# A fused attention and channel-mix kernel: first chunk's mixed gate inputs on ScalarE and GpSimd, first loads and due dates anew

## The chip, the cores and the metric

The kernel runs on one core of a Trainium2 chip. The metric is the device time of one execution in microseconds; lower is better. The kernel before takes 631.29 us (median of three runs, 630.67 to 632.04). The engines have the profile's names: PE is TensorE's matmul, PEld its weight load, DVE is VectorE, ACT is ScalarE, POOL is GpSimd, SP the engine that issues the DMAs.

## The reference

Inputs are q, k and v of shape (8, 8, 576, 64) (batch, heads, tokens, head size) and the weights of the second part. All is float32.

```python
k_p = k.reshape(B, H, 72, 8, 64).mean(axis=3)        # keys and values: means of 8 tokens
v_p = v.reshape(B, H, 72, 8, 64).mean(axis=3)
attn = softmax(q @ k_p.T / 8)                        # sum + 1e-9 below
x = (attn @ v_p) as (8, 576, 512)                    # heads side by side
xk = mu_k * x + (1 - mu_k) * x_prev                  # x_prev: the token before, 0 for the first
xr = mu_r * x + (1 - mu_r) * x_prev
s = maximum(xk @ w_k, 0) ** 2                        # 512 -> 1024
out = sigmoid(xr @ w_r) * (s @ w_v)                  # 512 -> 512, and 1024 -> 512
```

## The kernel before, in words

The 4608 tokens of the eight batches are cut into 12 chunks of 384, and each chunk into 3 tiles of 128 tokens (36 tiles). For every tile there is `softmax` (scores of four head pairs on PE at L620, their maximum, exponential and sum, and the products px and pm of exponentials and inverse sums; pm has 64 keys of each head, px the last 8), then `transposed` (pm, L695) and `transposed_rest` (px, L740). For every chunk follow `attended` for the four 128-wide slices g of x (L794: values times weights into a bank, with the tile of transposed weights pth and the rest ptr), `shifted` inside it (L807: ACT copies the bank twice, scaled by 1 - mu, one column to the right into t; GpSimd brings the carried column; L826: VectorE makes mu * bank + t), `hidden` for the eight 128-wide parts of the k multiply (L870, then relu on ACT at L880, the square), `gate` (L919, sigmoid at L926) and `mixed` (L951, the v multiply, multiplied with the gate at L960 and stored).

Chunk 0 is "whole": its multiplies take float32 operands, L826 writes straight into the operands xkh (for the k multiply, m = 0) and xrh (for the gate, m = 1). Later chunks split every operand into a high and a low half (`x_parts`: ACT casts at L842, GpSimd subtracts at L844; for weights `split`, L491 and L494) and multiply three times.

The weights come as 64-bit words and are converted to float32 by `convert`: one step on ACT (L460), three on VectorE (L462 a shift, L464, L469). There are 8 for k, 4 for r, 8 for v: the names wk0 to wk7, wr0 to wr3, wv0 to wv7. Keys and values are summed over 8 tokens in one of three ways by the table SUM_BY: "t" by 8 matmuls with the identity (L512, 16 records), "v" by three halving additions on VectorE and "g" by the same on GpSimd (both L501). k0 and k1 are the halves of batch 0's keys, v0 and v1 of its values, r0 their last 8 keys; k2, k3, v2, v3, r1 are those of batch 1. The q tiles are q0, q1 and so on. LOADS gives the order of the first loads; one SP queue issues them all, and with some eight under way each waits for an earlier one.

What runs when is set while the program is written: all these steps are threads with a due time, and a planner with rough costs of its own (class Order) picks for each engine the earliest due step that could start. EARLIER shifts the due time of single threads of the first chunks by some microseconds. The result is a fixed order on each engine; each engine works off its own queue in order, and a step that waits holds up all behind it. Scores have one double bank (sc), except tile 1 (BESIDE), which uses two of the three mm banks. Tiles in BY_HEAD have their exponentials made head by head on ACT with bias and sum in the same instruction (L642, eight each); for others VectorE subtracts the maximum (L651), ACT makes one exponential (L656), and VectorE sums (L658). Sigmoid and exponential need different tables on ACT; where they alternate the program has an ACT_TABLE_LOAD between them.

## Time and profile before

| | before |
|---|---|
| median of 3 runs | 631.29 us |
| lowest, highest | 630.67, 632.04 us |
| profiled execution | 631.28 us |
| its span, first to last instruction | 629.5 us |
| TensorE matmul busy | 615.7 us |
| VectorE, ScalarE, GpSimd busy | 402.1, 354.6, 208.2 us |
| ACT_TABLE_LOAD | 24, 1.28 us each |

The profile is of one execution on the chip. 631.28 is that execution's time and 629.5 the span of its instructions, so 1.8 us lie around the span. Busy time of PE is rough: a matmul's end is modelled, and records of matmuls that follow each other overlap. In a row of the timeline the first number is the start in microseconds from the span's start, the second the time that the row's instructions cover, and in square brackets stands how long the engine was idle ahead of it and what ended that. A row of the waits view gives who waited for whom: sum in microseconds, number of waits, longest. A row of the windows view gives a stretch, its length, the busy time (and the instructions) of PE, PEld, DVE, ACT and POOL, the clock granted to TensorE as a share of full speed, and the DMA engines' busy share and GB/s. A row of the groups gives the sum in microseconds, the mean in ns, and the idle time before. A float32 matmul has two records.

### The profile page before, as it was taken

The page shows a single profiled execution, that of the slowest core. Times are in us where ns is not written, and L with a number is a line of the kernel's source. Part 1 is how long each engine was busy: PE and PEld are TensorE (multiplying, and loading weights), DVE is VectorE, ACT ScalarE, POOL GpSimd, SP SyncE. Part 2 cuts the span into 40 slices and gives each one's busy share as a digit, 9 for nine tenths or more (in the row PEclk, how much of TensorE's full clock was granted, in tenths as well). Part 3 has the DMA queues.
Part 4 walks back from the last instruction along what each step waited for, and adds up shares of the span by engine and source line. Part 5 has one row for each costly group of instructions (what it writes and reads, how often), then busy time and mean ns, then how long its engine had stood idle before and what let it go on. Part 6 is the DMA issues. An engine that isn't in the chain of part 4 may idle for free.

```text
span 629.5 us, 8993 instructions
## 1 busy us (share of the span) xinstructions
PE 615.7 (98%) x3210; PEld 533.1 (85%) x3210; DVE 402.1 (64%) x786; ACT 354.6 (56%) x778; POOL 208.2 (33%) x324
## 2 busy tenths in 40 slices
PE   6899999999999999999999999999999999999997
PEld 5755459889889989989989988988988988988986
DVE  5999977857787458657735765844884643663421
ACT  4776666765675645645555564545575545564420
POOL 1130266453453048029024017305346005113100
PEclk9999999999999999999999999999999999999999
DMA  9995101123314211033001151001330100000001
GB/s 315 340 403 171 34 35 51 35 76 142 94 51 158 59 51 51 2 143 108 18 18 51 42 187 55 3 18 56 133 98 33 35 18 33 18 2 33 18 2 50
DMA packets 34989, 50.92 MB, mean 81 GB/s; under 512 B 6528, under 2 KB 22912, under 8 KB 34944
## 3 DMA queue, kind: packets, MB, share of 16 engines
q1 hardware_dynamic: 34944, 50.35, 23.9%
q8 instruction: 25, 0.41, 0.3%
q14 instruction: 20, 0.16, 0.1%
HBM read 40.90 MB, written 9.44 MB: 80 GB/s over the span
## 4 chain that ended last, share of the span: by engine, by line
PE 88%; DMA 6%; DVE 5%; SPq 1%; issue 0%; DVEq 0%
PE mm L951 32%; PE mm L870 29%; PE mm L919 14%; PE bank L794 5%; PE sc L620 5%; DMA got_wk<-in_w_k 4%; PE bank L695 2%; DMA got_wv<-in_w_v 1%; DVE tmp L464 1%; DVE got_wr L469 1%; PE bank L750 1%; SPq L421 0%; DVE got_wv L469 0%; DVE tmp L462 0%; DVE ptl L708 0%
## 5 line engine op out<-in xcount | busy, mean ns | idle before, releaser
L870 PE MATMUL mm<-xkh,w_k 128*128 128x384 f32 x704 | 182.3, 339 | 0.0
L951 PE MATMUL mm<-w_v,sh 128*128 128x512 f32 x528 | 171.7, 393 | 0.0
L870 PEld LDWEIGHTS mm<-xkh,w_k 128*128 128x128 f32 x704 | 125.6, 188 | 1.5 <-issue 0.6
L870 PE MATMUL mm<-xkl,w_k 128*128 128x384 f32 x352 | 118.0, 335 | 0.0
L951 PEld LDWEIGHTS mm<-w_v,sh 128*128 128x128 f32 x528 | 99.3, 188 | 19.5
L951 PE MATMUL mm<-w_v,sl 128*128 128x512 f32 x264 | 103.1, 390 | 0.0
L919 PE MATMUL mm<-w_r,xrh 128*128 128x512 f32 x264 | 86.3, 397 | 0.0
L807 ACT ACTIVATE t<-bank,om_sb 128x384 f32<-128x384 f32 x96 | 49.1, 580 | 46.7 <-PE bank L794 46.6
L893 ACT CAST sh<-rk 128x384 fp32r<-128x384 f32 x88 | 45.2, 513 | 51.9 <-DVE rk L887 51.4
L670 POOL TENSOR_TENSOR px<-e,sm 128x64 f32<-128x64 f32 x31 | 9.6, 310 | 189.8 <-DVE sm L664 189.8
L960 DVE TENSOR_TENSOR rs<-mm,rs 128x512 f32<-128x512 f32 x36 | 24.7, 687 | 74.7 <-PE mm L951 74.6
L826 DVE SCALAR_TENSOR_TENSOR xm<-bank,mu_sb,t 128x384 f32<-128x384 f32 x88 | 51.1, 612 | 31.8 <-POOL t L819 15.4
L895 DVE TENSOR_TENSOR sl<-rk,sh 128x384 fp32r<-128x384 f32 x88 | 53.3, 610 | 21.3 <-ACT sh L893 21.2
L870 PEld LDWEIGHTS mm<-xkl,w_k 128*128 128x128 f32 x352 | 66.1, 188 | 0.0
L887 DVE SCALAR_TENSOR_TENSOR rk<-mm,rk 128x384 f32<-128x384 f32 x88 | 48.5, 552 | 22.7 <-ACT rk L880 21.9
L501 POOL TENSOR_TENSOR stage<-stage 128x512 f32<-128x512 f32 (+5 forms) x60 | 52.9, 887 | 25.5 <-DMA stage<-in_vm 14.8
L844 POOL TENSOR_TENSOR xkl<-xm,xkh 128x384 fp32r<-128x384 f32 x44 | 45.5, 1034 | 48.0 <-ACT xkh L842 47.6
L919 PEld LDWEIGHTS mm<-w_r,xrh 128*128 128x128 f32 x264 | 49.7, 188 | 10.1
L951 PEld LDWEIGHTS mm<-w_v,sl 128*128 128x128 f32 x264 | 49.7, 188 | 8.9
L880 ACT ACTIVATE rk<-mm 128x384 f32<-128x384 f32 x88 | 42.9, 487 | 22.1 <-PE mm L870 21.1
L919 PE MATMUL mm<-w_r,xrl 128*128 128x512 f32 x132 | 51.5, 390 | 0.0
L620 PE MATMUL sc<-kbd,qs 128*128 128x144 f32 (+1 forms) x312 | 40.6, 289 | 5.4 <-ACT e L642 3.2
(120 smaller groups left out, 952.8 us busy)
## 6 DMA issues: line engine op xcount, KB each, us to landing
out<-rs SPq DMA_DIRECT2D x36, 256.0 KB, 2.0
stage<-in_kT SPq DMA_DIRECT2D x15, 576.0 KB, 4.9
qs<-in_qT SPq DMA_DIRECT2D x32, 256.0 KB, 3.3
stage<-in_vm SPq DMA_DIRECT2D x14, 512.0 KB, 5.4
got_wk<-in_w_k SPq DMA_DIRECT2D x8, 512.0 KB, 10.0
got_wv<-in_w_v SPq DMA_DIRECT2D x8, 512.0 KB, 10.1
stage<-in_vr SPq DMA_DIRECT2D x7, 384.0 KB, 4.2
got_wr<-in_w_r SPq DMA_DIRECT2D x4, 512.0 KB, 9.7
```

The lines of the kernel that those rows point to most:

```text
L501: nc_eng.tensor_tensor(out=st[:, :, :w], in0=st[:, :, :w], in1=st[:, :, w:2 * w], op=ALU.add)
L620: nc.tensor.matmul(out=halves[g // 2][o:o + n, 0, k:k + 2 * KEYS], lhsT=qs[:, g, o:o + n], rhs=kbd[b % 2][:, g, :], start=True, stop=True,)
L807: nc.scalar.activation(out=t[:, m, 1:n + 1], in_=xp, func=AF.Copy, scale=om_sb[:, m, g:g + 1])
L826: nc.vector.scalar_tensor_tensor(out=xm[:, :n], in0=xp, scalar=mu_sb[:, m, g:g + 1], in1=t[:, m, :n], op0=ALU.mult, op1=ALU.add,)
L844: nc.gpsimd.tensor_tensor(out=lo, in0=xm[:, :n], in1=hi, op=ALU.subtract)
L870: nc.tensor.matmul(out=hp, lhsT=w[:, o], rhs=x[:, ct, :n], start=(ct == 0 and k == 0), stop=(ct == NCT - 1 and k == len(terms) - 1),)
L880: nc.scalar.activation(out=rk[:, :n], in_=hp, func=AF.Relu)
L887: nc.vector.scalar_tensor_tensor(out=rk[:, :n], in0=hp, scalar=0.0, in1=rk[:, :n], op0=ALU.max, op1=ALU.mult)
L893: nc.scalar.copy(out=sh[:, :n], in_=rk[:, :n])
L895: nc.vector.tensor_tensor(out=operand("sl", c)[:, jt, :n], in0=rk[:, :n], in1=sh[:, :n], op=ALU.subtract)
L919: nc.tensor.matmul(out=bank, lhsT=x[:, ct, o], rhs=w, start=(ct == 0 and k == 0), stop=(ct == NCT - 1 and k == len(terms) - 1),)
L951: nc.tensor.matmul(out=bank, lhsT=s[:, o], rhs=w, start=(jt == 0 and k == 0), stop=(jt == NJT - 1 and k == len(terms) - 1),)
```

## The change

In chunk 0 (SCALED_ON_ACT) the mixed input of the gate, m = 1, is no longer one VectorE instruction: ACT writes mu * bank into xrh, and GpSimd adds t to it in place. The bank is given back after ACT's step, t after GpSimd's. BY_HEAD takes in tile 1, so all three tiles of chunk 0 have their exponentials by head. In SUM_BY k1 goes from VectorE to GpSimd, v0 from TensorE to VectorE, v2 from GpSimd to TensorE, r1 from GpSimd to VectorE. LOW_BY deals the low halves of the weights anew (k: one more on GpSimd, v: one less). LOADS has another order: k1 ahead of k0, q0 behind q1 and q2, the small constants ahead of wk0, r0, k3, q5 and k2 at other places. EARLIER, SPARE and SECOND (due times) are new throughout; of EARLIER's some 200 numbers two stand below.

```diff
 LOADS = (
-    "k0 k1 q1 q0 q2 wk0 c0 v0 v1 wk1 k3 r0 wk2 q3 wk3 wk4 v3 wk5 r1 q4 v2 wk6 wk7 wr0 wr1 q5 k2 wr2 "
+    "k1 k0 q1 q2 q0 c0 wk0 v0 r0 wk1 wk2 v1 k3 wk3 q3 wk4 r1 wk5 wk6 q4 v3 v2 q5 wk7 k2 wr0 wr1 wr2 "
     "wr3 wv0 wv1 wv2 wv3 wv4 wv5 wv6 wv7 "
 )
 SUM_BY = {
-    "k0": "t", "k1": "v", "v0": "t", "v1": "t", "r0": "t", "k2": "v", "k3": "v", "v2": "g", "v3": "v",
-    "r1": "g",
+    "k0": "t", "k1": "g", "v0": "v", "v1": "t", "r0": "t", "k2": "v", "k3": "v", "v2": "t", "v3": "v",
+    "r1": "v",
 }
-LOW_BY = {"k": "gvgvvvgv", "r": "gvgv", "v": "gvvggvgv"}
-BY_HEAD = (0, 2)
+LOW_BY = {"k": "gvgvvggv", "r": "gvvg", "v": "gvvvgvvg"}
+BY_HEAD = (0, 1, 2)
+SCALED_ON_ACT = (0,)
 EARLIER = {
-    "transposed_rest 6": 4.1, "hidden 2 5": -6.4, "convert r 1": -3.5, "mixed 0 1": -9.9,
+    "transposed_rest 6": -1.8, "hidden 2 5": -23.9, "convert r 1": -2.2, "mixed 0 1": -10.7,
...
-SPARE = 2.4
-SECOND = 13.3
+SPARE = 3.5
+SECOND = 12.9
...
-            yield "dve", 0.15 + n / 960, False
-            nc.vector.scalar_tensor_tensor(
-                out=xm[:, :n], in0=xp, scalar=mu_sb[:, m, g:g + 1], in1=t[:, m, :n],
-                op0=ALU.mult, op1=ALU.add,
-            )
-            if m == ms[-1] and last:
+            if m and c in SCALED_ON_ACT:
+                yield act(n)
+                nc.scalar.activation(out=xm[:, :n], in_=xp, func=AF.Copy, scale=mu_sb[:, m, g:g + 1])
+                order.give("bank", bank)
+                yield pool(n)
+                nc.gpsimd.tensor_tensor(out=xm[:, :n], in0=xm[:, :n], in1=t[:, m, :n], op=ALU.add)
                 order.give("t", t)
-                order.give("bank", bank)
+            else:
+                yield "dve", 0.15 + n / 960, False
+                nc.vector.scalar_tensor_tensor(
...
```

After the change the lines stand 2 later up to L826, and 11 later from the new branch on: L642 is L644, L651 is L653, L870 is L881, L926 is L937.

What this moves is seen in the order of the built program. First, ScalarE's queue from the first weight to the first tile's ptr. Before:

```order
L460 ACTIVATE tmp_102<-got_wk_138 128x512
L642 ACTIVATE e_88,sm_98<-sc_112,mx_96 128x72 x8
L656 ACTIVATE e_89<-e_89 128x576
L460 ACTIVATE tmp_101<-got_wk_155 128x512
L642 ACTIVATE e_88,sm_98<-sc_112,mx_96 128x72 x8
L747 CAST ptr_270<-bank_115 96x2x128
```

And now:

```order
L462 ACTIVATE tmp_102<-got_wk_142 128x512
L644 ACTIVATE e_88,sm_98<-sc_112,mx_96 128x72 x8
L644 ACTIVATE e_89,sm_99<-mm_118,mx_97 128x72 x4
L644 ACTIVATE e_89,sm_99<-mm_116,mx_97 128x72 x4
L583 CAST vq_100<-mm_117 96x128
L554 COPY vbd_w<-stage_108 64x2x64 x2
L644 ACTIVATE e_88,sm_98<-sc_112,mx_96 128x72 x8
L749 CAST ptr_289<-bank_115 96x2x128
```

Tile 1's single exponential became eight by head, and the second weight no longer stands between the tiles.

Second, TensorE from the last scores of the opening to the fourth slice of chunk 0's x. L512 sums values with the identity, L794 is `attended`, L870 (now L881) the k multiply; mm and bank are its banks. Before:

```order
L794 MATMUL bank_113<-pth_308,vbd_w 128x384
L794 MATMUL bank_113<-ptr_270,vbd_r_76 128x384
L870 MATMUL mm_117<-xkh_361,got_wk_165 128x384
L870 MATMUL mm_118<-xkh_361,got_wk_138 128x384
L794 MATMUL bank_115<-pth_308,vbd_w 128x384
L794 MATMUL bank_115<-ptr_270,vbd_r_76 128x384
L870 MATMUL mm_117<-xkh_361,got_wk_165 128x384
L870 MATMUL mm_118<-xkh_361,got_wk_138 128x384
```

And now:

```order
L796 MATMUL bank_115<-pth_295,vbd_w 128x384
L796 MATMUL bank_115<-ptr_289,vbd_r_76 128x384
L881 MATMUL mm_116<-xkh_362,got_wk_142 128x384 x2
L881 MATMUL mm_118<-xkh_362,got_wk_152 128x384 x2
L796 MATMUL bank_114<-pth_295,vbd_w 128x384
L796 MATMUL bank_114<-ptr_289,vbd_r_76 128x384
L796 MATMUL bank_113<-pth_295,vbd_w 128x384
L796 MATMUL bank_113<-ptr_289,vbd_r_76 128x384
L514 MATMUL mm_117<-stage_107,ident 128x128 x8
L881 MATMUL mm_116<-xkh_362,got_wk_142 128x384
```

Four k multiplies go ahead of the third slice, the third and fourth slices stand together, and the sums of v2 behind them. On VectorE there stand, ahead of the first mixed input (L837), the nine steps of weights 1, 2 and 4 and of softmax 3 (L464 three times, L466 and L471 twice each, a maximum L635 and a subtraction L653).

Third, ScalarE at the gates of chunk 0, where rs is the sigmoid's result and e an exponential's. Before:

```order
L460 ACTIVATE tmp_102<-got_wv_330 128x512
L926 ACT_TABLE_LOAD
L926 ACTIVATE rs_78<-mm_118 128x512
L460 ACTIVATE tmp_101<-got_wv_322 128x512
L926 ACTIVATE rs_79<-mm_116 128x512
L747 CAST ptr_457<-bank_113 96x2x128
```

And now:

```order
L462 ACTIVATE tmp_102<-got_wv_318 128x512
L937 ACT_TABLE_LOAD
L937 ACTIVATE rs_78<-mm_118 128x512
L658 ACT_TABLE_LOAD
L658 ACTIVATE e_88<-e_88 128x576
L462 ACTIVATE tmp_101<-got_wv_345 128x512
L462 ACTIVATE tmp_102<-got_wv_338 128x512
L937 ACT_TABLE_LOAD
L937 ACTIVATE rs_79<-mm_116 128x512
L658 ACT_TABLE_LOAD
L658 ACTIVATE e_89<-e_89 128x576
```

The exponentials of tiles 4 and 5, which stood ahead of the gates, stand between them; the whole program has 28 table loads where it had 24.

More of the change, by code (lines that the diff above doesn't have):

```diff
@@ L824, in shifted @@
                 xm = yield take("xm")
-            yield "dve", 0.15 + n / 960, False
-            nc.vector.scalar_tensor_tensor(
-                out=xm[:, :n], in0=xp, scalar=mu_sb[:, m, g:g + 1], in1=t[:, m, :n],
-                op0=ALU.mult, op1=ALU.add,
-            )
-            if m == ms[-1] and last:
-                order.give("t", t)
-                order.give("bank", bank)
+            if m and c in SCALED_ON_ACT:
[4 more added lines that the diff above has]
+                nc.gpsimd.tensor_tensor(out=xm[:, :n], in0=xm[:, :n], in1=t[:, m, :n], op=ALU.add)
+                order.give("t", t)
+            else:
+                yield "dve", 0.15 + n / 960, False
+                nc.vector.scalar_tensor_tensor(
+                    out=xm[:, :n], in0=xp, scalar=mu_sb[:, m, g:g + 1], in1=t[:, m, :n],
+                    op0=ALU.mult, op1=ALU.add,
+                )
+                if m == ms[-1] and last:
+                    order.give("t", t)
+                    order.give("bank", bank)
             if whole:
```

88 rows, old and new, of the table EARLIER are left out of this document.

## The prediction

> **What bounds the kernel now.** I read the page's first lines, then TensorE's waits over the whole span, then the windows view.
>
> ```profile
> span 629.5 us, 8993 instructions
> PE 615.7 (98%) x3210; PEld 533.1 (85%) x3210; DVE 402.1 (64%) x786; ACT 354.6 (56%) x778; POOL 208.2 (33%) x324
> ...
> PE sc L620 <- ACT e L642: 3.2, 1, 3.2
> PE mm L870 <- DVE xkh L826: 2.3, 2, 1.8
> PE bank L379 <- DVE tmp L375: 1.4, 1, 1.4
> PE sc L620 <- DMA qs<-in_qT: 1.4, 1, 1.4
> PE sc L620 <- DVE e L651: 0.8, 1, 0.8
> PE bank L740 <- DVE pr L732: 0.4, 1, 0.4
> PE mm L919 <- DVE got_wr L469: 0.2, 1, 0.2
> PE mm L951 <- DVE got_wv L469: 0.2, 1, 0.2
> ...
> 10.00:15.00 5.00, 1.81 (x14) 1.60 (x13) 4.48 (x14) 3.71 (x18) 0.00 (x0) 0.98 1.03 408
> 15.00:20.00 5.00, 5.00 (x33) 5.00 (x32) 4.93 (x20) 3.89 (x21) 0.00 (x0) 0.68 1.05 304
> 25.00:30.00 5.00, 2.92 (x10) 1.70 (x11) 4.97 (x10) 4.69 (x10) 1.31 (x5) 1.00 1.11 303
> 104.00:600.00 496.00, 495.94 (x2687) 449.04 (x2687) 310.26 (x590) 285.26 (x615) 172.99 (x267) 1.00 0.18 58
> ```
>
> From 104 to 600 us TensorE (first column after the length) is busy 495.94 of 496.00: there the end moves only if TensorE's work or its waits change. The waits sum to 9.9 us and all lie in the first 76 us; the 1.4 for L379 is the start-up, which nothing here touches, so 8.5 can go. One loss hides in busy time: the granted clock (third column from the right) is 0.68 in 15 to 20 us, after the 3.2 us wait.
>
> ```profile
> 14.84 3.55 PE L512 MATMUL mm<-stage,ident 128*128 128x128 f32 x16
> 18.44 1.95 PE L512 MATMUL mm<-early_sl,ident 128*128 128x128 f32 x16
> ```
>
> The same 16 records take 3.55 us there and 1.95 at full clock: 1.6 lost. So 10.1 us is all that can be won, and each microsecond by which TensorE waits more, anywhere, is lost.
>
> **The books.** TensorE's work stays the same: the sums of v0 (16 records) leave it and those of v2 (16 records) come to it. So the change of the time is the change of waits and slow clock. I carry the new order by hand with the durations of before up to the end of the first chunk's k multiplies, then look for new waits.
>
> **Opening.** The first tile's scores need both halves of the keys and q0.
>
> ```profile
> 4.79 2.20 PE L512 MATMUL mm<-stage,ident 128*128 128x144 f32 x16
> 6.10 1.60 DVE L501 TENSOR_TENSOR stage<-stage 128x576 f32<-128x576 f32 x3 [3.55 <-DMA stage<-in_kT]
> 8.34 1.22 PE L620 MATMUL sc<-kbd,qs 128*128 128x144 f32 x8 [1.35 <-DMA qs<-in_qT]
> 3.00 0.70 SPq L421
> 3.74 6.66 DMA got_wk<-in_w_k
> qs<-in_qT SPq DMA_DIRECT2D x1, 256.0 KB, 6.0
> L501 POOL TENSOR_TENSOR stage<-stage 128x512 f32<-128x512 f32 x1 | 1.3, 1269 | 0.0
> L501 POOL TENSOR_TENSOR stage<-stage 128x256 f32<-128x256 f32 x1 | 1.1, 1147 | 0.0
> ```
>
> k0 now lands second, at 6.1 instead of 4.7, so its sums end at 6.1 + 2.2 = 8.3. GpSimd adds up k1 from 4.7 on; it has no row with this tile. By 1.27 for 512 columns the first addition is 1.27 x 576/512 = 1.4, and the three between 2.6 (halving each time) and 3.6 (the small ones at the 1.15 and 1.0 that the row with 256 columns suggests): done at 7.3 to 8.3, behind TensorE's own sums either way, so I cost it at nothing; at 4.5 it would add 0.9. q0 is the third q, issued at 3.00 with 6.0 to landing: 9.05. Scores start at 9.1 instead of 8.34. The first weights, now behind the two small constants, land near 10.75 instead of 10.40, and the negation of the first maximum stands on VectorE behind their first shift: about 12.0 instead of 11.05.
>
> ```profile
> 10.42 0.66 ACT L460 ACTIVATE tmp<-got_wk 128x512 f32<-128x512 f32 x1 [2.06 <-DMA got_wk<-in_w_k]
> 11.14 0.32 ACT L642 ACTIVATE e<-sc,mx 128x72 f32<-128x72 f32 x1
> 13.43 0.24 ACT L642 ACTIVATION_READ_ACCUMULATOR e<-sc,mx 128x1 f32 x1
> 22.50 0.43 DVE L462 TENSOR_SCALAR tmp<-tmp 128x512 int32<-128x512 int32 x1 [1.26 <-ACT tmp L460]
> 23.41 0.69 DVE L676 TENSOR_TENSOR pm<-e,sm 128x512 f32<-128x512 f32 x1
> 25.55 0.91 PE L794 MATMUL bank<-pth,vbd_w 128*128 128x384 f32 x2
> 26.68 1.99 ACT L807 ACTIVATE t<-bank,om_sb 128x384 f32<-128x384 f32 x4
> 28.62 0.61 DVE L826 SCALAR_TENSOR_TENSOR xkh<-bank,mu_sb,t 128x384 f32<-128x384 f32 x1
> 29.29 1.56 PE L870 MATMUL mm<-xkh,got_wk 128*128 128x384 f32 x4 [1.82 <-DVE xkh L826]
> 40.18 0.60 DVE tmp L464
> ```
>
> Eight exponentials by head take 13.67 - 11.14 = 2.53 us on ScalarE. Now all three tiles do that: 12.1 to 14.65, 14.65 to 17.2, then two copies (0.8), 17.95 to 20.5; before, the third tile ended at 18.9. But before, VectorE then stood idle behind a weight's shift (L462, 1.26 us), and the third tile's products came at 23.41 to 24.10. Now no weight stands between, and at VectorE's pace (0.60 us from step to step for 512 columns, so 0.67 for 576) they end near 22.2. ScalarE is full from there: ten steps (small copies, weights 1 and 2, the transposed tiles) at some 0.43 us (the four t copies take 0.50 each, the small ones less) bring the last copy to 24.8, so values times weights (L794) start there instead of 25.55, the scaled copies t at 25.9 instead of 26.68, and VectorE, which now has weights 1 and 2, the shift of weight 4 and two steps of softmax 3 ahead (four of 0.60, three shifts of 0.34, two of 0.67: 4.8 from 22.9 on), reaches the first mixed input at 27.7 instead of 28.62. The first k multiply starts at **28.3 instead of 29.29: -1.0**. No gap of TensorE on this way is longer than 1.85 us, so I take full clock.
>
> But v0's sums were done before that point, and v2's now stand after it: **+1.8** (1.95 less the tail of the last record). They fill the wait for the third and fourth mixed inputs, the second of the two waits of L870: **-0.5** (2.3 - 1.8). At the end of the k multiplies the change is 0.3 us behind.
>
> The four r mixes: VectorE loses four of 0.61; ScalarE gets four, the like of L807 (1.99 for four), and GpSimd four additions of 384 columns, 1.00 to 1.59 by the rows of L844 below. Their results are wanted by the gates after 53 us and exist by 38, so they cost nothing; they hold the t tiles until 30.7 and 31.7 (by 1.59: 32.9), and the next t is written at 31.85 and 33.6.
>
> **Gates.** VectorE has less to do up to here: -1.60 (k1), -1.3 (softmax 1's subtractions and its sum, twice 576 columns), -2.4 (r mixes), +1.1 each for v0 and r1 (896 columns at its pace): about -3.1. It doesn't all arrive. ScalarE's preparation of weight r2 now stands behind the square of k multiply 5. The k multiplies go at some 2.6 each (four records 1.56, less the tail) from 37.9 on, and number 5, for which r2 waits, ends at 47.3; VectorE idles until 48.9, and has some 12.0 us of queue (six weights, k2's sums, softmax 4's maximum) up to softmax 4's subtraction, which frees the one score bank at 60.9. TensorE reaches softmax 5 at 59.8: k multiplies until 53.5, six gate steps of 0.87 (0.65 x 512/384), softmax 4 with 1.2.
>
> ```profile
> 54.53 0.75 DVE L651 TENSOR_TENSOR e<-sc,mx 128x576 f32<-128x576 f32 x1
> 55.34 1.25 PE L620 MATMUL sc<-kbd,qs 128*128 128x144 f32 x8 [0.81 <-DVE e L651]
> ```
>
> So the same kind of wait as before (0.8) comes back at 1.1, while the two of 0.2 for r and v weights go: **-0.1**.
>
> **Tables.** Each of the first two sigmoids is now followed by an exponential: four more table loads.
>
> ```profile
> 61.95 1.28 ACT L926 ACT_TABLE_LOAD   x1
> 63.24 0.60 ACT L926 ACTIVATE rs<-mm 128x512 f32<-128x512 f32 x1
> 90.09 1.59 POOL L844 TENSOR_TENSOR xkl<-xm,xkh 128x384 fp32r<-128x384 f32 x1 [0.64 <-ACT xkh L842]
> 93.37 1.00 POOL L844 TENSOR_TENSOR xkl<-xm,xkh 128x384 fp32r<-128x384 f32 x1 [0.32 <-ACT xkh L842]
> ```
>
> From load to sigmoid are 1.29 us, so 4 x 1.29 = 5.2 of ScalarE, which is 56% busy over the span. Softmax 4's exponential is done by 63.0 (load, sigmoid, load, exponential from 59.1 on), and VectorE takes its sum only at 63.6, five steps after the subtraction, so the cover is 0.6 us; beyond it, tile 4's transposition, which stands ahead of the first v multiply, makes TensorE wait. Nothing is added. [...]
>
> **Next chunks.** k multiplies of chunks 1 and 2 now start before all four mixed inputs of their chunk exist. The parts of the third and fourth come through one GpSimd queue, 1.00 to 1.59 each, with an addition of 1.27 ahead. TensorE may wait between nothing (the multiplies between cover 3 us) and 2.0 (both chunks, one slow part each): I take **+0.2**, since at the 1.00 of the last row nearly all of it is covered.
>
> Sum: -1.0 + 1.8 - 0.5 - 0.1 + 0.2 = +0.4. The profiled execution took 631.28, the median of the runs is 631.29: they are one number here. Forecast **631.7**, no difference that a measurement of this kernel (about 0.2%, 1.3 us) can tell.
>
> **The rivals.** *VectorE's relief arrives.* VectorE is busy 4.97 of 5 us in 25 to 30 and the change takes 3 us off it. If weight r2 isn't late, the wait at softmax 5 vanishes (-1.1), the 0.2 of the next chunks too, and the first multiply comes 1.0 earlier than I have it, since every one of its steps is a queue: 629.4. Against it: TensorE waited for VectorE only 1.2 us after 40. *The slow clock comes back.* Before, 1.81 us of work in 5 lost the clock, 2.92 didn't. After values times weights of two slices TensorE waits from 26.5 to 28.3; with the waits before it its worst 5 us hold 2.8 to 3.1 us of work. Below about 2.4 (the middle) the 16 records' price recurs at the first k multiplies: +1.6, 633.3, slower. [...] *The tables stall tile 4*, if softmax 4's exponential comes over 0.6 us late, with a load each time: 633 to 634. *The change doesn't relieve what it names*: the r mixes leave VectorE, but if it waits for ScalarE anyway nothing is seen; that is in my forecast.
>
> **Chances.** Forecast 0.47 (630.0 to 632.5), VectorE's relief 0.28, slow clock 0.14, tables or chunk waits 0.11. Slower than 632.5: 0.25. The range takes in the relief with some tenths beyond, and the slow clock with 0.7 of chunk waits: 628.8 to 634.0. It leaves out the full 2.0 of chunk waits on top.
>
> **What would show it.** Right: first score multiply near 9.1, exponentials of three tiles unbroken from 12.1 to 20.5, first k multiply at 28.3, clock 1.00 in 10 to 30 us, a wait of TensorE for e L653 (L651 before) near 1 us at softmax 5. Wrong: the first k multiply a microsecond off, a window with a clock under 0.9 after 10 us, a wait at the first L881 of chunks 1 or 2 over 1 us, or waits beyond 104 us, where there are none now.

## The result, and the profile after

| | before | after |
|---|---|---|
| median of the runs compared | 631.20 us | 640.02 us |
| lowest, highest (4 runs each) | 630.67, 632.04 | 638.71, 640.60 |
| profiled execution, its span | 631.28, 629.5 us | 640.30, 638.5 us |

The change makes the kernel slower: the ratio after/before is 1.0127, with a 95% interval of 1.0098 to 1.0156. The time lies outside the predicted range.

The first lines of the page after, and TensorE's waits over the whole span (sum, number, longest):

```profile
span 638.5 us, 9025 instructions
PE 620.7 (97%) x3210; PEld 533.9 (84%) x3210; DVE 399.8 (63%) x783; ACT 364.1 (57%) x801; POOL 209.5 (33%) x325
...
PE mm L881 <- DVE xkh L837: 1.8, 1, 1.8
...
PE bank L697 <- DVE pr L732: 1.4, 1, 1.4
PE mm L514 <- DMA early_sl<-in_vr: 1.4, 1, 1.4
PE mm L514 <- POOL stage L503: 1.3, 1, 1.3
PE mm L881 <- DVE rk L898: 1.3, 3, 0.5
PE sc L622 <- DVE e L653: 1.1, 1, 1.1
PE mm L930 <- DVE rk L898: 0.9, 1, 0.9
PE mm L881 <- POOL xkl L855: 0.6, 2, 0.5
...
PE mm L881 <- ACT xkh L853: 0.5, 1, 0.5
```

TensorE has as many matmuls as before, and its waits no longer all lie in the opening: the waits for rk (what the relus of the k multiplies leave, and what frees their banks), for xkl and for ScalarE's xkh are new. The windows view tells where; a row of before stands ahead of each row of after:

```profile
130.00:180.00 50.00, 50.00 (x279) 44.99 (x278) 35.82 (x73) 33.38 (x68) 19.84 (x25) 1.00 0.29 90
130.00:180.00 50.00, 46.91 (x258) 41.31 (x257) 40.01 (x77) 33.28 (x73) 26.22 (x34) 1.00 0.25 76
180.00:600.00 420.00, 419.97 (x2274) 381.06 (x2273) 254.67 (x479) 232.68 (x503) 142.11 (x228) 1.00 0.17 55
180.00:600.00 420.00, 419.65 (x2259) 378.93 (x2258) 242.40 (x466) 230.30 (x497) 139.99 (x224) 1.00 0.17 55
```

From 130 to 180 us, which is chunk 2, TensorE was never idle before and now is for 3.1 us, while GpSimd works 26.2 us there in place of 19.8 and VectorE 40.0 in place of 35.8. From 180 us on there is little to tell apart.

Idle time alone misses slow clock, and the tails of the records ahead of each wait. So I also counted lost time: for each TensorE record the time to the start of the next, less the smallest median that its shape has in any of the runs (matmuls that an experiment adds are counted as lost). Against before, after loses **3.8** us from 0 to 130 us, **4.7** from 130 to 180, and 0.6 later; together 9.1, and the spans differ by 9.0. The same three numbers stand with each experiment below; they are of its one profiled execution, while the medians are of all its runs.

**The opening.** TensorE after, start and duration first:

```profile
6.51 3.79 PE L514 MATMUL mm<-stage,ident 128*128 128x144 f32 x16 [1.28 <-POOL stage L503]
10.95 1.25 PE L622 MATMUL sc<-kbd,qs 128*128 128x144 f32 x8 [0.65 <-ACT kbd L539]
14.57 1.99 PE L514 MATMUL mm<-early_sl,ident 96*96 96x128 f32 x16 [1.39 <-DMA early_sl<-in_vr]
29.64 4.54 PE L881 MATMUL mm<-xkh,got_wk 128*128 128x384 f32 x8 [1.79 <-DVE xkh L837]
35.66 1.95 PE L514 MATMUL mm<-stage,ident 128*128 128x128 f32 x16
...
30.00:40.00 10.00, 10.00 (x40) 6.36 (x38) 8.12 (x19) 6.02 (x15) 3.06 (x8) 0.83 1.04 398
```

k0's sums take 3.79 where they took 2.20, so the scores start at 10.95. r0's sums, which stand ahead of tile 2's scores, wait until r0 has landed. The first k multiplies start at 29.64 and take 4.54, at a granted clock of 0.83 over that window; at full clock (in the run with r0 first, below) the same eight records take 2.85, so 1.7 is lost there. VectorE, which the forecast had idle until 48.9 us ahead of softmax 5, is busy from 40 to 50 us (the third number after the length), and 9.92 of the next 10 us:

```profile
40.00:50.00 10.00, 9.96 (x34) 5.83 (x33) 10.00 (x18) 8.42 (x18) 2.19 (x2) 1.00 1.02 407
```

**Chunk 2.** TensorE in before and then in after: the last values times weights of the chunk, its first k multiply, and of after the waits that follow.

```profile
136.82 0.34 PE L794 MATMUL bank<-ptr,vbd_r 96*128 96x384 f32 x1
143.32 0.60 PE L870 MATMUL mm<-xkh,w_k 128*128 128x384 f32 x2
...
150.54 0.34 PE L796 MATMUL bank<-ptr,vbd_r 96*128 96x384 f32 x1
150.71 0.51 PE L881 MATMUL mm<-xkh,w_k 128*128 128x384 f32 x2
154.54 0.62 PE L881 MATMUL mm<-xkh,w_k 128*128 128x384 f32 x2 [0.54 <-ACT xkh L853]
155.62 0.44 PE L881 MATMUL mm<-xkl,w_k 128*128 128x384 f32 x1 [0.46 <-POOL xkl L855]
...
163.17 0.62 PE L881 MATMUL mm<-xkh,w_k 128*128 128x384 f32 x2 [0.54 <-DVE rk L898]
...
172.19 0.50 PE L930 MATMUL mm<-w_r,xrh 128*128 128x512 f32 x1 [0.87 <-DVE rk L898]
```

Before, the fourth slice of x was ready 6.5 us ahead of the first k multiply. Now the third and fourth come right ahead of it, and the multiplies of the first two slices cover 3.3 us in which four scaled copies, mixed inputs, casts and subtractions must be made. The inputs come 0.5 late twice, and then the relus run late: six waits above 0.2 us in all, 3.1 together. On VectorE after, the maximum and the subtraction of tile 12 stand ahead of these mixed inputs:

```profile
150.75 0.75 DVE L635 TENSOR_REDUCE mx<-sc 128x8 f32<-128x576 f32 x1
151.54 0.76 DVE L653 TENSOR_TENSOR e<-sc,mx 128x576 f32<-128x576 f32 x1
...
153.33 1.66 DVE L837 SCALAR_TENSOR_TENSOR xm<-bank,mu_sb,t 128x384 f32<-128x384 f32 x3
...
152.19 0.30 POOL L817 COPY t<-carry 128x2 f32<-128x2 f32 x2
```

Not all of the delay is theirs: the last row is GpSimd's carried column, which the mixed inputs need and which was copied only from 152.19 to 152.49, behind an addition. With VectorE free the first of them could have started less than 1 us sooner by these rows, where tile 12's two steps take 1.5.

VectorE is also slowed in this stretch. GpSimd's and VectorE's rows that overlap, and the same VectorE step beside an idle GpSimd last:

```profile
130.95 1.29 POOL L496 TENSOR_TENSOR w_v<-got_wv,w_v 128x512 fp32r<-128x512 f32 x1 [7.98 <-ACT w_v L493]
131.18 1.08 DVE L663 TENSOR_SCALAR sm<-sm 128x8 f32<-128x8 f32 x1
...
143.08 0.17 DVE L663 TENSOR_SCALAR sm<-sm 128x8 f32<-128x8 f32 x1
```

A step of 0.17 us lasts 1.08 and ends when GpSimd's step ends (132.25). Summing what VectorE's steps take over the lower quartile of their line and shape gives 3.2 us in 130 to 150 us after, and 0.1 before; from 150 to 180 us there is no such difference (2.9 and 3.2).

### The profile page after: what moved, and what is told of

It is laid out like the page before. It is cut to its first block, busy times and chain, and to the rows that moved or that the text cites. A ratio compares the mean times of both kernels' runs of the same rounds, so it can differ in the third digit from the quotient of the medians.

```text
span 638.5 us, 9025 instructions
## 1 busy us (share of the span) xinstructions
PE 620.7 (97%) x3210; PEld 533.9 (84%) x3210; DVE 399.8 (63%) x783; ACT 364.1 (57%) x801; POOL 209.5 (33%) x325
## 4 chain that ended last, share of the span: by engine, by line
PE 77%; DVE 12%; ACT 5%; POOL 3%; issue 2%; DMA 1%; POOLq 0%; DVEq 0%; ACTq 0%
PE mm L962 27%; PE mm L881 25%; PE mm L930 14%; PE bank L796 5%; PE sc L622 4%; PE bank L697 2%; DVE tmp L466 1%; DVE sm L660 1%; DVE xm L837 1%; DVE sl L906 1%; DVE mx L635 1%; PE mm L514 1%; POOL xrl L855 1%; POOL xkl L855 1%; POOL stage L503 1%
## 5 line engine op out<-in xcount | busy, mean ns | idle before, releaser
L881 PE MATMUL mm<-xkh,w_k 128*128 128x384 f32 x704 | 181.7, 338 | 1.8 <-DVE rk L898 1.3
L881 PEld LDWEIGHTS mm<-xkh,w_k 128*128 128x128 f32 x704 | 125.5, 188 | 4.2 <-DVE rk L898 2.4
L881 PE MATMUL mm<-xkl,w_k 128*128 128x384 f32 x352 | 118.2, 336 | 0.6 <-POOL xkl L855 0.6
L962 PEld LDWEIGHTS mm<-w_v,sh 128*128 128x128 f32 x528 | 99.2, 188 | 19.9 <-issue 0.2
L930 PE MATMUL mm<-w_r,xrh 128*128 128x512 f32 x264 | 85.0, 395 | 0.9 <-DVE rk L898 0.9
L837 DVE SCALAR_TENSOR_TENSOR xm<-bank,mu_sb,t 128x384 f32<-128x384 f32 x88 | 51.1, 613 | 40.0 <-POOL t L821 24.5
L906 DVE TENSOR_TENSOR sl<-rk,sh 128x384 fp32r<-128x384 f32 x88 | 54.7, 624 | 29.0 <-ACT sh L904 28.8
L881 PEld LDWEIGHTS mm<-xkl,w_k 128*128 128x128 f32 x352 | 66.1, 188 | 1.6 <-POOL xkl L855 1.6
L635 DVE TENSOR_REDUCE mx<-sc 128x8 f32<-128x576 f32 x35 | 26.3, 752 | 48.5 <-PE sc L622 48.4
L891 ACT ACTIVATE rk<-mm 128x384 f32<-128x384 f32 x88 | 42.9, 489 | 19.8 <-PE mm L881 15.9
L503 POOL TENSOR_TENSOR stage<-stage 128x512 f32<-128x512 f32 (+8 forms) x57 | 49.2, 871 | 4.2 <-DMA stage<-in_kT 2.2
L678 POOL TENSOR_TENSOR pm<-e,sm 128x512 f32<-128x512 f32 x31 | 32.6, 1052 | 54.0 <-PE bank L697 48.4
```

What stands on the lines that cost most here:

```text
L503: nc_eng.tensor_tensor(out=st[:, :, :w], in0=st[:, :, :w], in1=st[:, :, w:2 * w], op=ALU.add)
L635: nc.vector.tensor_reduce(out=mx if len(svs) == 1 else mx[:, a:a + 1], in_=sv, axis=AX.X, op=ALU.max)
L837: nc.vector.scalar_tensor_tensor(out=xm[:, :n], in0=xp, scalar=mu_sb[:, m, g:g + 1], in1=t[:, m, :n], op0=ALU.mult, op1=ALU.add,)
L881: nc.tensor.matmul(out=hp, lhsT=w[:, o], rhs=x[:, ct, :n], start=(ct == 0 and k == 0), stop=(ct == NCT - 1 and k == len(terms) - 1),)
L891: nc.scalar.activation(out=rk[:, :n], in_=hp, func=AF.Relu)
L906: nc.vector.tensor_tensor(out=operand("sl", c)[:, jt, :n], in0=rk[:, :n], in1=sh[:, :n], op=ALU.subtract)
```

## The experiments

Each number pair is median and ratio [95% interval] against the kernel before on the same chip; "lost" is the three stretches, of one execution. The names e1 to e18 in the expectations are the experiments' labels, which stand in brackets behind their titles here. Line numbers move a little from kernel to kernel: the k multiply is L870 to L884.

### Due dates

**After, with chunks 2 and 3 dated as before** (e1; two of the numbers):

```diff
-    "attended 2 2": -19.7, "attended 2 3": -3.0,
+    "attended 2 2": -22.3, "attended 2 3": -4.2,
...
-SPARE = 3.5
-SECOND = 12.9
+SPARE = 2.4
+SECOND = 13.3
```

> The changed kernel with the due dates of chunks 2 and 3 (and of the keys and values of batches 2 and 3), SPARE and SECOND of before. Nothing differs up to tile 7's scores, some 105 us in. TensorE's order has attended 2 0 and 2 1 ahead of the v multiply of tile 1 of chunk 1 again, and attended 2 2 and 2 3 ahead of that of tile 2, 8 multiplies earlier than in the changed kernel, with one tile's scores between instead of three. Theory A (late dates: the mixed inputs of slices 2 and 3 and VectorE's queue come too late for chunk 2's k multiplies): the waits for rk, xkh and xkl between 130 and 200 us go, 640.0 - 4.9 = 635.1. Rival B (the opening, or ScalarE's and GpSimd's new work, makes all later work late): the waits stay or move, 639 to 640.5.

638.61, 1.0108 [1.0081, 1.0136]; lost 3.6, 3.4, 0.4. In chunk 2 the waits for xkh and xkl are gone, and another stands in their place. TensorE, ScalarE and GpSimd, and the window around them:

```profile
155.32 0.62 PE L881 MATMUL mm<-xkh,w_k 128*128 128x384 f32 x2 [1.90 <-DVE rk L898]
...
153.55 0.60 ACT L554 CAST vbd_h<-stage 64x128 fp32r<-64x128 f32 x2 [2.41 <-POOL stage L503]
...
150.88 4.27 POOL L503 TENSOR_TENSOR stage<-stage 128x512 f32<-128x512 f32 x5
...
155.00:160.00 5.00, 4.68 (x18) 4.68 (x19) 4.75 (x11) 2.38 (x6) 2.74 (x5) 0.67 0.00 0
```

GpSimd sums a batch's values; ScalarE's cast of them waits 2.41 us; the relus stand behind the cast, so the k multiplies find no bank; and the clock falls to 0.67. The dates do set which wait chunk 2 has, but giving back the old ones doesn't give back the old order; the planner starts from another first chunk.

**The same without SPARE and SECOND** (e2)**:**

> As the first run, but SPARE and SECOND stay as in the changed kernel: the due dates alone go back. TensorE's order still has attended 2 2 and 2 3 behind all multiplies of chunk 1 and directly ahead of chunk 2's k multiplies, but one tile's scores less ahead of them (10, not 12). If the place of attended 2 2 and 2 3 is the cause: the loss between 130 and 200 us stays, 4 to 5 us, 639.5. If it is the scores of tiles 10 to 12 ahead of them on VectorE (three steps of some 0.75 us for each tile): most of it goes, 636.

640.29, 1.0137 [1.0107, 1.0167]; lost 2.5, 2.7, 3.0. From 130 to 260 us its waits for rk sum to 2.8 (longest 1.7). A good part of the loss moves on past 180 us.

**Chunk 1 dated as before too** (e5)**:**

> The changed kernel with the due dates of chunks 1, 2 and 3 (and batches 2 and 3), SPARE and SECOND of before: chunk 0 and the weights alone stay as changed. TensorE has attended 2 2 inside the v multiply of tile 1 of chunk 1 and attended 2 3 right behind it, ahead of tile 2's eight multiplies, as before. Theory A (late dates): the excess of TensorE's steps over their usual length between 130 and 200 us, 6.7 in the changed kernel and 1.7 before, comes to 2, and the time is near 635 to 636. Rival B (ScalarE's and GpSimd's queues in chunks 1 and 2 are worse off because of chunk 0's new work and order): a wait for rk, xkh or xkl of 1 us or more stays, 637 to 640.

643.47, 1.0194 [1.0173, 1.0214]; lost 7.5, 4.1, 0.4: worse than either theory had it, with new waits at 102.7 (for xkl, 1.7) and 130.1 (for pr, 2.2), each followed by slow clock (pairs of k multiplies on xkh take 0.84 from 104.31 on where the same take 0.51 from 107.65 on; pairs of the gate take 1.06 at 131.81 and 133.09 where they took 0.63 at 123.40). Here only chunk 0 and the weights stay as changed, and 130 to 180 us still loses 4.1.

**Before, with after's dates of chunks 2 and 3, SPARE and SECOND** (e6)**:**

> The kernel before with the due dates of chunks 2 and 3 (and batches 2 and 3), SPARE and SECOND of the changed kernel; the opening, SUM_BY, BY_HEAD, LOADS and the place of the gate's mixed inputs stay as before. attended 2 2 and 2 3 come later than in either kernel, inside chunk 2's first k multiplies. Theory A: waits for rk, xkh or xkl appear between 130 and 200 us and nowhere earlier, 4 to 6 us in all, some 636. Rival B (dates cost nothing without the new work of chunk 0): 631 to 633.

646.20, 1.0235 [1.0213, 1.0258]; lost 3.9, 7.7, 1.8. TensorE's waits from 130 to 180 us:

```profile
PE mm L870 <- POOL xkl L844: 3.3, 4, 1.9
PE mm L870 <- ACT xkh L842: 1.4, 3, 0.8
PE mm L870 <- DVE rk L887: 0.8, 2, 0.6
```

These are kinds of wait that after has too, but in other shares: more for the inputs (4.7, where after has 1.0), less for rk (0.8 and 1.8). So the dates alone, with nothing of the change in the first chunk, are enough for a loss in chunk 2. The expectation was off by 10 us all the same: the loss in chunk 2 is larger than it had, and 3.9 us go ahead of 130 us, where it had none; the k multiplies of chunk 1 wait 2.2 us for rs (the product with the gate), and the granted clock from 45 to 130 us is 0.98, where before has 1.00.

**SPARE alone, in before (3.5; e16) and in after (2.4; e17):**

```diff
-SPARE = 2.4
+SPARE = 3.5
```

> The kernel before with SPARE 3.5 instead of 2.4 and nothing else: the time by which the planner keeps softmax, transposed and attended of chunks 2 and later off TensorE grows by 1.1 us. Orders are the same up to tile 8's scores, some 110 us in; then attended 2 0 and 2 1 stand at the end of tile 1's v multiply of chunk 1 and 2 2 and 2 3 at the end of tile 2's. If the later place of attended costs by itself: new waits for xkl, rk or pr from 110 to 200 us of 2 to 6 us, 634 to 638. If the dates of before carry it: within 1 us of before.

> The changed kernel with SPARE 2.4 instead of 3.5 and nothing else. attended 2 0 and 2 1 come 1 multiply earlier and 2 2 and 2 3 3 and 1 multiplies earlier than in the changed kernel, with the scores of one tile less ahead of them. If SPARE makes the loss in chunk 2: the excess from 130 to 200 us falls from 6.7 to 3 or less, 1.0127 - 0.006 = 1.007 times before. If any new order there costs as much: 1.010 to 1.015.

Before with 3.5: 635.70, 1.0061 [1.0039, 1.0082]; lost in the profiled execution (the fastest of 11) −0.3, 1.2, 1.6. One number of the planner's is worth 0.6%. After with 2.4: 639.55, 1.0111 [1.0082, 1.0139]; lost 3.8, 2.4, 1.5, with waits for pr (2.1) in place of xkh: no gain.

**The dates of the first experiment, and the values of batch 3 held back** (e10) until the k multiply "hidden 2 3", so that GpSimd's sums don't stand ahead of the cast:

```diff
+        if b == 3:
+            yield need(("hid", 2, 3))
```

> As e1 (before's dates for chunks 2 and 3), and the sums of batch 3's values may not start before the k multiply's part 3 of chunk 2 is done. In e1 a copy of these sums stood in ScalarE's queue ahead of chunk 2's first relu and waited 2.4 us for GpSimd; TensorE then waited 1.9 us for rk and lost 1.7 us of clock. Theory A (attended 2 2 and 2 3 early enough and nothing ahead of the relu): no wait from 130 to 200 us over 0.3 us, the excess there 2 (1.7 before, 6.7 in the changed kernel), 1.0127 - 0.0075 = 1.005 times before. Rival B (VectorE and ScalarE are too full in chunk 2 after the new chunk 0, whatever the order): another wait of over 1 us takes its place, 1.009 or more.

641.01, 1.0148 [1.0123, 1.0174]; lost 5.0, 5.2, 0.4. The wait for the cast is gone, but now VectorE meets GpSimd's sums:

```profile
157.33 2.24 DVE L734 CAST pr<-px 128x64 fp32r<-128x64 f32 x1 [2.79 <-POOL px L674]
...
158.25 5.83 POOL L503 TENSOR_TENSOR stage<-stage 128x512 f32<-128x512 f32 x6
...
160.09 0.62 PE L883 MATMUL mm<-xkh,w_k 128*128 128x384 f32 x2 [1.57 <-DVE rk L900]
```

A cast that elsewhere takes 0.18 lasts 2.24, the steps that make rk stand behind it, and TensorE waits again.

### The mixed inputs of the gate

**Before, with SCALED_ON_ACT** and the program planned anew (e7):

> The kernel before with the named part of the change alone: in chunk 0 ScalarE makes mu * bank of the gate's mixed inputs and GpSimd adds t; all tables and dates stay as before. If the part costs nothing: within 1 us of before. If it brings VectorE's relief: 0.5 to 1.5 less, with the waits at 29 and 37 us shorter. If ScalarE's four more steps and GpSimd's four additions stand in the way (rival B): 1 to 3 more.

637.94, 1.0112 [1.0087, 1.0137]; lost 5.8, −0.3, 0.3: 6.9 us more, where 1 to 3 were the worst expected. The loss is all in the first 130 us; chunk 2 keeps what it was.

**The same in before's own order** (e9), the new instructions standing where VectorE's step stood:

```diff
+            if m and c == 0:
+                nc.scalar.activation(out=xm[:, :n], in_=xp, func=AF.Copy, scale=mu_sb[:, m, g:g + 1])
+                nc.gpsimd.tensor_tensor(out=xm[:, :n], in0=xm[:, :n], in1=t[:, m, :n], op=ALU.add)
```

> The kernel before with the named part of the change, as in e7, but with the planner's books kept as if VectorE still made these mixed inputs: every engine's order stays that of before, and only the four instructions themselves move (ScalarE mu * bank, GpSimd adds t). In e7 the planner rearranged the rest, and it cost 6.9 us. Theory A (the new order cost it, not the operation): within 1 us of before; since VectorE is busy 29.8 of 30 us from 30 to 60, its four steps of 0.61 less may bring up to 1.4 (waits at 37, 55, 60 and 71 us): 629.6 to 631. Rival B (ScalarE's and GpSimd's steps cost it): 4 to 7 us more.

636.34, 1.0074 [1.0053, 1.0094]; lost 5.0, −0.3, 0.3. VectorE's two weight shifts, and GpSimd beside them:

```profile
31.16 4.82 DVE L462 TENSOR_SCALAR tmp<-tmp 128x512 int32<-128x512 int32 x2
...
30.93 2.13 POOL L501 TENSOR_TENSOR stage<-stage 96x512 f32<-96x512 f32 x2
33.03 0.86 POOL L828 TENSOR_TENSOR xrh<-xrh,t 128x384 f32<-128x384 f32 x1
...
34.43 1.26 POOL L501 TENSOR_TENSOR stage<-stage 128x512 f32<-128x512 f32 x1
```

In before, the two shifts take 0.71 together:

```profile
32.49 0.71 DVE L462 TENSOR_SCALAR tmp<-tmp 128x512 int32<-128x512 int32 x2
```

Here they last 4.82, beside GpSimd's work from 30.93 to 35.69, and the second ends at 35.98, 0.29 after GpSimd stops. The third mixed input stands behind them: TensorE waits 3.7 for xkh in all (2.3 before) and 1.3 for ScalarE's relu.

**The same, with the addition on VectorE** (e12)**:**

```diff
-                nc.gpsimd.tensor_tensor(out=xm[:, :n], in0=xm[:, :n], in1=t[:, m, :n], op=ALU.add)
+                nc.vector.tensor_tensor(out=xm[:, :n], in0=xm[:, :n], in1=t[:, m, :n], op=ALU.add)
```

> The kernel before in its own order, as e9, but of the gate's mixed inputs in chunk 0 ScalarE makes mu * bank and VectorE (not GpSimd) adds t. In e9 VectorE's shift of a weight stood at 31.2 us and two of these, 0.42 each elsewhere, ended at 36.0, as GpSimd's back-to-back additions ended at 35.7. Theory P (GpSimd's additions hold up VectorE): no such stretch, 0 to 1.5 more than before (VectorE may wait for ScalarE's product). Rival S (ScalarE's product in its queue is the cost): 3 to 5 more, as e9's 4.7.

633.17 (11 runs), 1.0013 [1.0000, 1.0026]; lost 1.5, −0.3, 1.1. The two shifts take 0.71 again. So ScalarE's half of the edit, with the addition on VectorE, costs 0 to 1.6 us by the interval, and the addition on GpSimd most of the 4.7.

**Before, with four additions on GpSimd whose results nothing reads** (e14)**:**

```diff
+            if m and c == 0:
+                nc.gpsimd.tensor_tensor(out=unread[:, :n], in0=xm[:, :n], in1=xm[:, :n], op=ALU.add)
```

> The kernel before as it is, and four more additions of 384 columns on GpSimd, at the places that e9 has, into a tile that nothing reads; nobody waits for them, ScalarE has nothing new and t is given back as before. Theory P (VectorE cannot start some of its steps while GpSimd works on memory): VectorE's shifts of weights between 30 and 42 us are stretched by 1 us or more again, and 1 to 4 more than before. Rival T (in e9 the t tiles and banks came back later, through ScalarE and GpSimd): within 0.7 of before.

636.33, 1.0076 [1.0049, 1.0103]; lost 4.3, −0.4, 0.4. VectorE, GpSimd, ScalarE and TensorE:

```profile
31.33 3.67 DVE L463 TENSOR_SCALAR tmp<-tmp 128x512 int32<-128x512 int32 x2
...
33.44 1.27 POOL L502 TENSOR_TENSOR stage<-stage 128x512 f32<-128x512 f32 x1
...
42.31 0.60 ACT L553 CAST vbd_h<-stage 64x128 fp32r<-64x128 f32 x2 [7.11 <-POOL stage L502]
...
43.48 2.85 PE L873 MATMUL mm<-xkh,got_wk 128*128 128x384 f32 x8 [1.62 <-ACT sh L883]
```

Nobody waits for these additions, and yet the kernel loses nearly as much as in the run before last. The price is not in the data: it is in what VectorE can't do meanwhile (the two shifts take 3.67 where they take 0.71 in before), and in GpSimd's own sums behind them, for which ScalarE's cast waits 7.11, and the relu behind that, and TensorE 1.62 for the relu. No run tells the two apart.

**After in its own order, with the r mixes back on VectorE** (e13), and **after with SCALED_ON_ACT empty** (e15), planned anew:

```diff
-                nc.scalar.activation(out=xm[:, :n], in_=xp, func=AF.Copy, scale=mu_sb[:, m, g:g + 1])
+                nc.vector.scalar_tensor_tensor(
+                    out=xm[:, :n], in0=xp, scalar=mu_sb[:, m, g:g + 1], in1=t[:, m, :n],
+                    op0=ALU.mult, op1=ALU.add,
+                )
...
-                nc.gpsimd.tensor_tensor(out=xm[:, :n], in0=xm[:, :n], in1=t[:, m, :n], op=ALU.add)
```

> The changed kernel, every engine's order kept, but VectorE makes the gate's mixed inputs of chunk 0 again (one instruction each, where ScalarE's product stood in the program); ScalarE and GpSimd have nothing of it. If the named part itself costs in the changed kernel as it did in e9: 635 to 638, 1.004 to 1.009 times before, less from 30 to 60 us. If its cost was hidden there by the order (v2's sums and the v multiplies fill the waits): 638.5 to 641, with VectorE's four steps of 0.61 more; the loss from 130 to 180 us stays 4 to 5 in either case.

> The changed kernel with SCALED_ON_ACT empty: VectorE makes all mixed inputs, and the planner orders anew; LOADS, SUM_BY, BY_HEAD and due dates stay as changed. Tells what the rest of the change costs. attended 2 2 and 2 3 still stand directly ahead of chunk 2's k multiplies, with tiles 10 and 11's scores ahead of them (in the changed kernel 10 to 12). If the named part is most of the loss: 633 to 635. If the due dates are: 637 to 640, with 4 us lost between 130 and 180 us.

641.22, 1.0143 [1.0120, 1.0166], lost 4.9, 4.6, 0.6; and 640.00, 1.0121 [1.0100, 1.0143], lost 4.4, 3.1, 1.2. Without the part that names the change, the loss is the same: in the changed kernel it costs nothing that can be told. A likely reason, which no run tests, is that v2's sums have gone from GpSimd to TensorE and r1's to VectorE: GpSimd works 3.06 of the 10 us from 30 to 40 us, where in before it works 5.94, and there is little for the additions to hold up.

### Opening and clock

**After with six warming matmuls in place of four** (e3; WARMING, matmuls of a constant ahead of the first data):

> The changed kernel with six warming matmuls instead of four; every engine's order is otherwise the same. They end near 6.1 instead of 5.23, so TensorE waits some 0.4 instead of 1.28 us ahead of k0's sums. Theory C (that wait has the clock at half): k0's 16 records take 2.2 instead of 3.8 us, the first scores start near 9.3 instead of 10.95, the first k multiply between 28.1 and 28.9 (29.64 less 0.8 to 1.6), 638.4 to 639.2. Rival D (the clock is at half there because TensorE has not worked for long enough since the start, and two more matmuls don't change that): 3.8 us stay, 640. Rival E (the third tile and the r0 values, landed at 14.5, bound the way to the first k multiply): k0's sums at full clock, but the first k multiply near 29.6 and 640.

639.83, 1.0124 [1.0098, 1.0150]; lost 2.3, 4.7, 0.6. k0's sums take 2.12 and the scores start at 9.37, but r0's sums still start at 14.23, and tile 2's scores behind them at 16.06. The gain of 1.6 in the first scores ends in a longer wait for r0 (2.63 in place of 1.39), and the slow clock shows up elsewhere (the eight score records at 24.06 take 2.13 where those at 16.06 take 1.15): the first k multiply starts at 29.53.

**After with eight matmuls of the identity ahead of the first k multiply** (e4), which nothing reads:

```diff
+            if c == 0 and jt == 0 and ct == 0:
+                for _ in range(8):
+                    nc.tensor.matmul(out=bank[:, :P], lhsT=ident, rhs=ident, start=True, stop=True)
```

> The changed kernel with eight more matmuls of the identity with itself (128 columns, some 0.22 us each) into the bank of the first k multiply, ahead of it, so that TensorE works in the wait of 1.79 us for the first mixed input; their results are overwritten. Every engine's order is otherwise the same. Theory F (that wait costs the clock): the k multiplies from 31.2 to 33.7 run at full clock, 1.6 us less, 638.4. Rival G (they run at half clock for the work of the many microseconds before, and the wait alone doesn't decide): 640.

639.93, 1.0121 [1.0095, 1.0147]; lost 4.2, 4.7, 0.7. The k multiplies go at full clock (2.79 for the eight records), but in this execution r0's sums go at slow clock (3.21 where they take 1.99): no gain that can be told.

**After with six warming matmuls and r0 loaded ahead of v0** (e11)**:**

```diff
-    "k1 k0 q1 q2 q0 c0 wk0 v0 r0 wk1 wk2 v1 k3 wk3 q3 wk4 r1 wk5 wk6 q4 v3 v2 q5 wk7 k2 wr0 wr1 wr2 "
+    "k1 k0 q1 q2 q0 c0 wk0 r0 v0 wk1 wk2 v1 k3 wk3 q3 wk4 r1 wk5 wk6 q4 v3 v2 q5 wk7 k2 wr0 wr1 wr2 "
```

> The changed kernel with six warming matmuls (as e3) and r0 loaded ahead of v0; every engine's order is otherwise that of the changed kernel. In e3 k0's sums ran at full clock and the scores came 1.6 us earlier, but TensorE then waited 2.6 us for r0 (landed at 14.2), and tile 2's scores stood behind it. Theory E (the landing of r0 bounds tile 2): r0 lands near 12.5, the wait is 1 us, tile 2's scores start at 14.5 instead of 16.06 and its exponentials at 17.5 instead of 18.33; first k multiply 28.6 to 28.8, 1.0127 - 0.0014 = 1.011. Rival I (VectorE's steps and the tables of weights bound the way from there): tile 2 earlier, first k multiply within 0.3 of 29.5, 1.0125.

638.90, 1.0118 [1.0088, 1.0147]; lost 0.8, 4.7, 0.6 in the profiled execution, the fastest of four. TensorE:

```profile
12.46 1.99 PE L514 MATMUL mm<-stage,ident 96*96 96x128 f32 x16 [0.97 <-DMA stage<-in_vr]
...
28.34 2.85 PE L881 MATMUL mm<-xkh,got_wk 128*128 128x384 f32 x8 [1.79 <-DVE xkh L837]
```

With r0 two microseconds earlier, and a granted clock of 1.000 over this execution, the first k multiply starts at the 28.3 of the forecast. Chunk 2 still loses its 4.7, and over all four runs no gain can be told from after's 1.0127.

**Before, with 13 matmuls of the identity ahead of tile 2's scores and 8 at the first k multiplies** (e8), and then **the 13 alone** (e18)**:**

```diff
+        if i == 2:
+            for _ in range(13):
+                nc.tensor.matmul(out=spare_bank[:, :P], lhsT=ident, rhs=ident, start=True, stop=True)
+            order.give("bank", spare_bank)
```

> The kernel before with more matmuls of the identity with itself, 128 columns each, whose results nothing reads: 13 ahead of tile 2's scores (the wait of 3.2 us) and 8 ahead of the first k multiply (the wait of 1.8 us); every engine's order is otherwise the same. Theory F (stretches in which TensorE works less than half cost it the clock for some 3.4 us): no slow stretch from 14.8 to 18.0 us, and the first k multiply comes up to 1.6 us earlier if the way leads over TensorE; 629.5 to 631, and the runs lie closer together. Rival H (the lost 1.6 us is hidden, since VectorE's queue leads to the first k multiply): clock 1.00, the first k multiply still at 29.3, and the same time as before.

> The kernel before with the 13 more matmuls of e8 in the wait for tile 2's scores, and without the 8 at the k multiplies, which in e8 stood behind the first k multiply and took 1.8 us themselves. In e8 v0's sums ran at full clock and the first k multiply came at 27.8 instead of 29.3. Theory F (the way to the first k multiply leads over TensorE's half clock): first k multiply at 27.8 again and 0.5 to 1.5 us less than before, 0.998 to 0.9992 times. Rival H (VectorE, busy 29.8 of 30 us from 30 to 60, takes the 1.5 us back): first k multiply at 27.8, longer waits at 37 and 55 us, the same time as before.

631.20, 0.9995 [0.9982, 1.0009], lost −0.2, 0, −0.1: the eight stood behind the first k multiply, where nothing was to fill, and took back what the 13 won. The 13 alone: **630.71** (12 runs), 0.9979 [0.9965, 0.9993], lost −0.8, 0, 0. TensorE there:

```profile
15.05 1.95 PE L512 MATMUL mm<-stage,ident 128*128 128x128 f32 x16
...
28.18 1.56 PE L875 MATMUL mm<-xkh,got_wk 128*128 128x384 f32 x4 [1.82 <-DVE xkh L831]
```

v0's sums take 1.95 in place of 3.55 and the k multiplies start 1.1 earlier. This is the one version that beats the kernel before, by about 1.2 us (0.4 to 2.2 by the interval).

## Why the prediction was wrong

**The step that failed most: "Next chunks ... I take +0.2", with bounds of 0 and 2.0.** It measured 4.7 (130 to 180 us) in place of it. Of the 8.6 us between forecast and measured change (+0.4 and 9.0), 4.5 are this term, 1.7 the slow clock at the first k multiplies and 1.3 their later start; where the other 1.1 go is left open. The mechanism was named there (k multiplies that start before all mixed inputs of their chunk exist, with 3 us of multiplies as cover), but it was sized by GpSimd's queue alone, and as a wait at the entry. In chunk 1 it cost nearly nothing, as I had it. In chunk 2 tile 12's softmax stands ahead on VectorE, the inputs come 1.0 late in all, and TensorE waits for rk three more times, 1.8 together: the entry is the smaller part. That the one leads to the other is read from the trace. The front of this document calls EARLIER, SPARE and SECOND new throughout; I followed them only up to 60 us and at two later points. That they are enough for a loss is shown: in before, SPARE alone makes it 0.6% slower and the late dates 2.35%. That they are what costs it in after is not: with the dates of chunks 1 to 3 put back the stretch still lost 4.1. In the runs that change the dates, or keep after's, chunk 2 loses 1.2 to 7.7 us; in those that keep before's dates (the four with the r mixes changed or unread additions, and the two fills) it loses nothing. How the loss of that stretch divides between tile 12's place and slow VectorE steps is left open: VectorE's steps drawn out beside GpSimd are read from the trace, and no run takes them away alone; undoing the dates in after only brought other waits, so what a kernel with after's first chunk and a good order of chunk 2 would take stays open.

**"No gap of TensorE on this way is longer than 1.85 us, so I take full clock".** Wrong by 1.7 in the profiled execution. The rival of the slow clock put 1.6 at the first k multiplies, and that is where it came. Its measure, TensorE's work in 5 us with a border near 2.4, doesn't tell it, though: from 25 to 30 us TensorE works 2.86 in after, which lost the clock, and 2.92 in before, which didn't. It isn't a fixed cost either: the first two experiments, with the same order up to there, had full clock at the k multiplies (2.85 for the eight records in both, and a granted clock of 1.00 from 30 to 40 us). The first (e1) starts them at 29.67, as after does, and its last v multiply of chunk 0 at 95.76, where after has 97.47: the 1.7 is there. It loses 1.5 of it again by 130 us, mostly at waits in chunk 1 that after doesn't have; from some 105 us on its order is another.

**"First k multiply at 28.3".** It came at 29.64. What failed in it is k0's sums at full clock: they took 3.79, and the scores came at 10.95, not 9.1. The exponentials start at 13.50 instead of 12.1, and from there ScalarE has no idle time until those of the third tile, which ran from 19.1 to 21.4 and not from 17.95 to 20.5. A second thing was hidden behind this: r0, whose landing at 14.5 I didn't carry at all, though its sums stand ahead of tile 2's scores. With k0's sums at full clock alone (e3) the third tile's exponentials wait for it, until 18.33. With both mended (e11) they start at 17.87, the third tile's products end at 22.3 (forecast 22.2), the first mixed input comes at 27.68 (27.7) and the first k multiply at 28.34: the rest of that chain was right.

**What held.** v2's sums in front of the k multiplies took 1.95, as priced at +1.8; the second wait for xkh is gone (−0.5); the tables make no wait at tile 4. VectorE's relief never arrived, as the forecast had it. Softmax 5 waits 1.1 for e, the number forecast, but that is luck: the wait was to come from VectorE idling until 48.9 for weight r2, and VectorE is busy 19.9 of the 20 us from 40 to 60; the scores start at 64.56 and not at 60.9, and both sides of the difference moved by as much.

**The r mixes "cost nothing".** Right in the changed kernel as far as the runs can tell (two versions without them are as slow), and right that the change doesn't relieve what it names. But the reason given, that their results are wanted late, was not enough: in before's order they cost 4.7 us, and unread additions 4.4, with no reader at all. The term to count was what GpSimd holds up, not when its result is read.

**What the sum missed as a whole.** "10.1 us is all that can be won" was right as a bound on one side; no bound stood on the other, where a kernel whose TensorE is 100% busy from 104 us on has only cover to lose.

## What to carry to other kernels

A step that goes to GpSimd is priced by what VectorE does at that moment and by what stands behind it on GpSimd, not by when its result is read (in before's order the additions cost most of 4.7 us with a reader, and 4.4 without). Where a table of dates feeds a greedy planner, list for each later stretch what now stands ahead of every input of the busiest engine, to the end of the stretch and not only at its entry; a date put back doesn't bring back the old order. And look for spans of some 3.4 us in which TensorE works less than half (1.04 us ahead of the slow clock in before, 1.62 in after): a few matmuls that nothing reads can be cheaper than the slow clock behind them, if they stand in the gap itself (0.2% here).

## What the runs showed of the hardware

**The clock fell behind stretches that TensorE worked less than half.** In the traces' record of the granted clock the slow stretch of before (14.76 to 18.18) and that of after (30.25 to 33.66) last 3.41 us each at 0.50, and within one execution the clock's changes lie whole multiples of 3.41 us apart (after: it rises at 9.77 and at 33.66, seven of them; before: at 4.52 and 18.18, four). Laid as a grid over these two traces, from the first rise to the end, four cells were worked less than half by TensorE, and each was followed by slow clock: the one ahead of 14.76 in before (30.5%), the one ahead of 30.25 in after (47.5%), and those ahead of the ends, 629.15 in before (0.3%) and 637.82 in after (10.6%). All others were worked 59% or more, and none of them was followed by slow clock. The border isn't sharp in these numbers: TensorE works 1.62 of 3.41 us both in after from 26.83 on and in the first experiment from 26.95 on, with a wait of 1.79 in both, and only after lost the clock (4.54 for the eight records of the k multiplies, 2.85 in the first experiment). What decides at the border the traces don't tell. At the start, the four warming matmuls (3.8 us) didn't always raise the clock in time: k0's sums took 3.79 in after, whose cell from 2.94 on was worked 67%, and 2.20 in before, whose cell from 1.11 on was worked 90%.

**VectorE's steps lasted longer beside GpSimd's.** Two shifts that take 0.71 us together in before lasted 4.82 beside GpSimd's work in the run in before's own order (e9), and 3.67 in the one with unread additions (e14). Each time the second ended 0.29 us after GpSimd stopped (35.98 behind 35.69, and 35.00 behind 34.71); in e9 GpSimd had gone through seven instructions from 30.93 on by then. With the addition on VectorE (e12) they take 0.71 again. In after a step of 0.17 lasted 1.08 and ended with GpSimd's, at 132.25. It isn't every step: in e14 a mixed input on VectorE at 30.11 took 0.61, as elsewhere, while GpSimd added from 29.88 to 31.94. What holds the longer ones the traces don't show.
